# One attention-then-MoE kernel: a fixed GpSimd order, token numbers inside the sorted rows, two-head blocks for the last queries, and transposing DMAs for the MoE input

## The chip, the cores and the metric

One Trainium2 chip, one of its NeuronCores. The metric is device time in microseconds of one execution of the whole kernel. Engines are named as in the profile: PE (TensorE), PEld (its weight loads), DVE (VectorE), ACT (ScalarE), POOL (GpSimd), SP (SyncE). DMAs issued by POOL run in the software queue q0, those issued by SP in the hardware queue q1; both use the core's 16 DMA engines.

## The reference, cut to what matters

```python
# q, k, v: (8, 8, 576, 64); hidden 32
scores = q @ k.T / 8
pos = np.arange(S)
psi_rel = np.log1p(np.abs(pos[:, None] - pos[None, :]))
psi_i = np.log1p(np.maximum(pos[:, None], 1.0))
bias = np.maximum((psi_rel / psi_i)[..., None] @ w1 + b1, 0.0) @ w2     # (576, 576, 8 heads)
attn = softmax(scores + bias.transpose(2, 0, 1))
x = (attn @ v).transpose(0, 2, 1, 3).reshape(4608, 512)                 # tokens
for e in range(8):                                                      # one domain, one expert
    mask = domain_id == e
    out[mask] = np.maximum(x[mask] @ w1[e], 0.0) @ w2[e]                # 512 -> 1024 -> 512
```

## The kernel before, in words

**Stages.** The kernel runs five stages in turn. (1) Constants: `L4` holds logarithms of distances, `slope` one factor for each query row. (2) Position bias (`_phase_bias`): in 9 blocks `ib` of 64 queries, 16 tiles `hr` each (hidden units of 4 queries by 576 keys, 144 tiles in all, 36 buffers), PE multiplies them with `W2BIG` into `eb`, ACT evicts `eb` into the bias tables with Exp. (3) Routing (`_phase_route`): DVE computes for each token its row `posi` in an order sorted by expert (640 rows for each expert, a spill area behind). (4) Attention over 8 batches, 21 units each: PE writes scores `sc`, ACT takes the Exp into `e`, DVE multiplies by the bias, PE sums with v into `pu`, DVE normalizes (`norm`). Keys and queries 512 to 575 of each head are handled apart (`xl`, the last 64 queries). After the fourth head pair the finished rows `xt` are scattered by POOL's indirect DMAs into `fire_x`, a tensor in DRAM in sorted order, 4 scatters of 128 tokens and one of 64 for each batch. (5) MoE: for each expert 640 rows of `fire_x` are read as `xg`, transposed on PE into `xT`, then 64 matmuls into `hps` (Relu on ACT gives `hT`) and 40 into `ops`; DVE copies to `res`, and POOL scatters 5 blocks of 128 rows to the output by `sidx`, the token numbers of the sorted rows.

**Where `sidx` comes from.** `_phase_route` fills a DRAM tensor `fire_perm` by 40 indirect DMAs that write one 4-byte token number for each token, and reads it back once.

**What sets the order.** PE, DVE and ACT run in the order of the code. POOL's and SP's instructions are placed by the scheduler of the framework. One sequence of DMAs matters on SP: the zero fill of `fire_x` stands ahead of the second load of the domain numbers (`dom`), which the routing waits for. The expert weights come in through POOL (f32 to f16 in the DMA), two DMAs for each expert; experts 0 to 2 into the pool `wsb`, 3 to 6 into `wsb2`, 7 into `wsb` again.

Of the kernel before, what the change touches and what calls it, by code (L numbers as in the profile page):

```python
# [9 lines left out]
F32 = mybir.dt.float32  # L10
F16 = mybir.dt.float16
# [9 lines left out]
B = 8  # L21
# [9 lines left out]
PAD = 1 << 20  # L31

# [23 lines left out]
def _no_order(tc, key, inst):  # L56

    ins = inst.ins if hasattr(inst, "ins") else inst
    tc.declare_no_dep(ins, group=key, reason="rows of one permutation")
    tc.add_to_no_dep_group(key, ins)  # L60


def _setup_constants(tc, G, w1, b1, w2):
# [12 lines left out]
    nc.sync.dma_start(out=w1col, in_=bass.AP(tensor=w1.tensor, offset=0, ap=[[0, 4], [1, 32], [1, 1]]))  # L76
    G.nb1 = cst.tile([P, 1], F32, tag="nb1", name="nb1")
    nc.sync.dma_start(out=G.nb1, in_=bass.AP(tensor=b1.tensor, offset=0, ap=[[0, 4], [1, 32], [1, 1]]))
    nc.vector.tensor_scalar(out=G.nb1, in0=G.nb1, scalar1=-1.0, scalar2=None, op0=AO.mult)
# [9 lines left out]
    si = cst.tile([P, NGR], I32, tag="si", name="si")  # L89
    li = G.tmp.tile([P, W4 + W1], I32, tag="li", name="li")  # L90
    for g in range(4):
        pg = slice(32 * g, 32 * g + 32)

        nc.gpsimd.iota(si[pg, 0:128], base=4 * g, channel_multiplier=0, pattern=[[1, 4], [16, 32]])
        nc.gpsimd.iota(si[pg, 128:144], base=512 + g, channel_multiplier=0, pattern=[[4, 16]])
        nc.gpsimd.iota(li[pg, 0:W4], base=-(C4 + 4 * g), channel_multiplier=0, pattern=[[1, W4]])
        nc.gpsimd.iota(li[pg, W4:], base=-(C1 + 512 + g), channel_multiplier=0, pattern=[[1, W1]])
    G.slope = cst.tile([P, NGR], F32, tag="slope", name="slope")
    nc.vector.tensor_copy(out=G.slope, in_=si)
    nc.vector.tensor_scalar(out=G.slope, in0=G.slope, scalar1=1.0, scalar2=None, op0=AO.max)  # L100
    nc.scalar.activation(out=G.slope, in_=G.slope, func=AF.Ln, bias=1.0, scale=1.0)
    nc.vector.reciprocal(out=G.slope, in_=G.slope)
    nc.vector.tensor_scalar(out=G.slope, in0=G.slope, scalar1=w1col[:], scalar2=None, op0=AO.mult)
    lf = G.tmp.tile([P, W4 + W1], F32, tag="lf", name="lf")
    nc.vector.tensor_copy(out=lf, in_=li)
    nc.vector.scalar_tensor_tensor(out=lf, in0=lf, scalar=-1.0, in1=lf, op0=AO.mult, op1=AO.max)
    G.L4 = cst.tile([P, W4 + W1], F16, tag="L4", name="L4")
    nc.scalar.activation(out=G.L4, in_=lf, func=AF.Ln, bias=1.0, scale=1.0)  # L108


def _phase_bias(tc, G):
# [3 lines left out]
    with tc.tile_pool(name="fsb", bufs=1, side="right") as fsb, \  # L115
         tc.tile_pool(name="fps", bufs=1, space=bass.MemoryType.PSUM) as fps:
        for ib in range(9):
            hrl = []
            for k16 in range(16):
                if ib < 8:  # L120
                    r, a = ib // 2, 16 * (ib % 2) + k16
                    m, c0 = 32 * r + a, C4 - (16 * a + r)
                else:
                    m, c0 = 128 + k16, W4 + C1 - 4 * k16
                hr = fsb.tile([P, S], F16, tag="hr", name="hr", bufs=36)
                nc.vector.tensor_scalar(out=hr, in0=G.L4[:, c0: c0 + S],  # L126
                                        scalar1=G.slope[:, m: m + 1], scalar2=G.nb1[:],
                                        op0=AO.mult, op1=AO.max)
                hrl.append(hr)
            for jcs in ((0, 1), (2, 3), (4,)):  # L130
                eb = fps.tile([P, 2, 512], F32, tag="eb", name="eb", bufs=3)
                for k16 in range(16):
                    for lj, jc in enumerate(jcs):
# [5 lines left out]
                        else:  # L139
                            for h2 in range(2):  # L140
                                nc.tensor.matmul(
                                    out=eb[64 * h2: 64 * h2 + 64, lj, 32 * k16: 32 * k16 + 32],
                                    lhsT=hr[:, 512:576], rhs=G.W2BIG[:, 0:32], start=True, stop=True)
                ebv = eb.rearrange("p l (i h) -> p l h i", h=8)
                i0 = 64 * ib
                if jcs[0] == 4:
                    for h2 in range(2):
                        o = G.biasR[64 * h2: 64 * h2 + 64, :, i0: i0 + 64] if ib < 8 else \
                            G.biasRL[64 * h2: 64 * h2 + 64]
                        nc.scalar.activation(out=o, in_=ebv[64 * h2: 64 * h2 + 64, 0, h2::2, :],  # L150
# [16 lines left out]
def _phase_route(tc, G, moe_domain_id):  # L167
# [8 lines left out]
    G.perm_dram = nc.dram_tensor("fire_perm", (NSLOT, 1), I32, kind="Internal").ap()  # L176
# [100 lines left out]
    padt = pbuf.tile([P, NSLOT // P], I32, tag="padt", name="padt")  # L277
    nc.gpsimd.memset(padt, PAD)
    nc.sync.dma_start(out=G.perm_dram.rearrange("(p c) o -> p (c o)", p=P), in_=padt)
    nidx = pbuf.tile([P, B, NT], I32, tag="nidx", name="nidx")  # L280
    nc.gpsimd.iota(nidx[:, :, 0:4], base=0, channel_multiplier=4, pattern=[[S, B], [1, 4]])
    nc.gpsimd.iota(nidx[:, :, 4], base=512, channel_multiplier=1, pattern=[[S, B]])
# [8 lines left out]
    G.sidx = pbuf.tile([P, E * NCH, 1], I32, tag="sidx", name="sidx")  # L291
    nc.sync.dma_start(out=G.sidx, in_=bass.AP(tensor=G.perm_dram.tensor, offset=0,
                                              ap=[[1, 128], [128, E * NCH], [1, 1]]))


class _Attention:
# [443 lines left out]
```

## Time and profile before

| | us |
|---|---|
| median of 3 runs (range) | 527.84 (526.59 to 532.48) |
| the profiled execution, its own time | 523.68 |
| its span, first to last instruction | 522.0 |
| busy PE / DVE / ACT / POOL | 373.6 / 260.3 / 231.1 / 202.0 |

The profiled execution is 4.2 us under the median of the runs; its span is 1.7 us under its own time. No engine is busy for more than 72% of the span, and the shares are averages over stages with different limits: a stage is read by which wait ends last in it. Times in the rows further down count from the start of the span.

### The profile page before, as it was taken

How to read it: one execution, taken by the hardware profiler on the slowest of the kernel's cores; microseconds unless marked ns; L12 is line 12 of the kernel's file. 1: busy time of each engine (PE TensorE's matmuls, PEld its weight loads, DVE VectorE, ACT ScalarE, POOL GpSimd, SP SyncE). 2: the span in 40 equal slices, each digit the busy share in tenths (PEclk: the TensorE clock that was granted, in tenths of full speed). 3: DMA queues.
4: the chain of work that ended last, by engine and by line, in shares of the span. 5: the costliest groups of instructions: out<-in, count | busy, mean ns of one | idle time of the engine just before them, and what ended most of it. 6: DMA issues, size and time to landing. Idle time of an engine off the chain costs nothing. (4 is left out here: it accounts for less than half of the span.)

```text
span 522.0 us, 10886 instructions
## 1 busy us (share of the span) xinstructions
PE 373.6 (72%) x4578; PEld 235.3 (45%) x4578; DVE 260.3 (50%) x572; ACT 231.1 (44%) x290; POOL 202.0 (39%) x238
## 2 busy tenths in 40 slices
PE   0578844311298988889898977079639999999992
PEld 0366733100055555465555544055425566566550
DVE  5899985100369695777768674013022422422411
ACT  1444521000388987889697875021402143143140
POOL 9740445777606546543403042603013303313312
PEclk9999999555599999999897989579959999999997
DMA  0999987000992999979401010899998313102211
GB/s 3 155 233 366 319 123 131 2 0 0 99 155 53 161 203 149 151 124 114 77 3 46 4 46 21 160 241 241 215 246 206 112 50 123 69 22 88 81 39 73
DMA packets 79034, 61.39 MB, mean 118 GB/s; under 512 B 23558, under 2 KB 71430, under 8 KB 78984
## 3 DMA queue, kind: packets, MB, share of 16 engines
q0 software_dynamic: 56576, 45.12, 49.7%
q1 hardware_dynamic: 22408, 15.57, 10.8%
q8 instruction: 36, 0.59, 0.4%
q14 instruction: 14, 0.11, 0.1%
HBM read 67.17 MB, written 25.49 MB: 177 GB/s over the span
## 5 line engine op out<-in xcount | busy, mean ns | idle before, releaser
L412 ACT ACTIVATE e<-sc 128x1024 f16<-128x1024 f32 x168 | 156.7, 998 | 93.5 <-remote 67.2
L605 ACT ACTIVATE hT<-hps 128x640 f16<-128x640 f32 x64 | 45.1, 704 | 137.8 <-PE hps L601 136.2
L570 POOL DMA_INDIRECT out_dram<-res,sidx x40 | 39.5, 988 | 132.6 <-DVE res L569 131.9
L566 PE MATMUL ops<-w2e,hT 128*128 128x512 f16 x320 | 71.5, 383 | 0.0
L601 PE MATMUL hps<-xT,w1e 128*128 128x320 f16 x512 | 71.2, 300 | 0.0
L385 PE MATMUL sc<-qkT 64*128 64x512 f16 x256 | 54.3, 407 | 22.7 <-ACT e L412 16.7
L477 POOL DMA_INDIRECT fire_x<-xt,posi x32 | 34.4, 1076 | 81.2 <-DVE xt L459 71.0
L569 DVE COPY res<-ops 128x512 f32<-128x512 f32 x40 | 27.7, 691 | 76.2 <-PE ops L566 51.0
L417 DVE TENSOR_TENSOR e<-e,biasM 128x1024 f16<-128x1024 f16 x96 | 63.4, 685 | 3.3 <-ACT e L412 3.0
L601 PEld LDWEIGHTS <-w1e 128*128 128x128 f16 x512 | 50.3, 98 | 20.7
L136 PE MATMUL eb<-W2BIG,hr 128*128 128x32 f16 x576 | 36.0, 196 | 25.8 <-DVE hr L126 18.8
L433 PE MATMUL pu<-vext,e 128*128 128x65 f16 x1024 | 53.0, 199 | 0.0
L126 DVE TENSOR_SCALAR hr<-L,slope,nb 128x576 f16<-128x576 f16 x144 | 51.6, 435 | 1.7 <-ACT L L108 1.7
L561 DVE COPY xT<-pxt 128x512 f16<-128x512 f16 x40 | 15.8, 421 | 65.8 <-PE pxt L559 64.1
L566 PEld LDWEIGHTS <-hT 128*128 128x128 f16 x320 | 31.3, 99 | 36.8 <-issue 1.4
L287 POOL DMA_INDIRECT fire_perm<-nidx,posi x40 | 38.7, 969 | 21.0 <-issue 21.0
L433 PEld LDWEIGHTS <-e 128*128 128x128 f16 x1024 | 46.2, 102 | 0.0
L367 DVE COPY qkT<-pt 128x1024 f16<-128x1024 f16 x32 | 21.8, 683 | 47.7 <-remote 43.5
L136 PEld LDWEIGHTS <-hr 128*128 128x128 f16 x576 | 26.5, 117 | 34.7 <-DVE hr L126 17.6
L429 PE MATMUL pu<-vrag,e 128*128 128x130 f16 x128 | 29.9, 234 | 13.1 <-DVE xl L470 7.9
L559 PE MATMUL pxt<-idn,xg 128*128 128x128 f16 x160 | 15.1, 235 | 33.6 <-DMA xg<-fire_x 18.1
L345 PE MATMUL pt<-idn,qn 128*64 128x128 f16 x256 | 15.3, 249 | 27.1 <-DVE qkT L367 14.3
(123 smaller groups left out, 407.6 us busy)
## 6 DMA issues: line engine op xcount, KB each, us to landing
fire_x<-zero SPq DMA_DIRECT2D x1, 9984.0 KB, 37.0
w1e<-in_moe_w_dram POOLq DMA_DIRECT2D x8, 1024.0 KB
w2e<-in_moe_w_dram POOLq DMA_DIRECT2D x8, 1024.0 KB
xg<-fire_x SPq DMA_DIRECT2D x8, 640.0 KB, 8.6
qn<-in_q_dram POOLq DMA_DIRECT2D x8, 512.0 KB
kn<-in_k_dram POOLq DMA_DIRECT2D x8, 512.0 KB
vst<-in_v_dram POOLq DMA_DIRECT2D x8, 512.0 KB
fire_perm<-nidx,posi POOLq DMA_INDIRECT x40
```

The costliest lines, as they stand in the source:

```text
L126: nc.vector.tensor_scalar(out=hr, in0=G.L4[:, c0: c0 + S], scalar1=G.slope[:, m: m + 1], scalar2=G.nb1[:], op0=AO.mult, op1=AO.max)
L136: nc.tensor.matmul(out=eb[:, lj, 32 * k16: 32 * k16 + 32], lhsT=rap(hr, jc, [[4, 128]]), rhs=G.W2BIG[:, 0:32], start=True, stop=True)
L287: _no_order(tc, "slots", nc.gpsimd.indirect_dma_start(out=G.perm_dram[:, :], out_offset=bass.IndirectOffsetOnAxis(ap=G.posi[0:n, c:c + 1], ...
L385: mm(out=sc[:, h2, :], lhsT=self.qkT[b, p][hs[h2], 1, 128 * c: 128 * c + 128], rhs=self.qkT[b, p][hs[h2], 0, :], start=not raw, stop=True)
L412: nc.scalar.activation(out=ef[:, 0:n], in_=sf[:, 0:n], func=AF.Exp, bias=0.0, scale=0.125)
L417: self.nc.vector.tensor_tensor(out=job[0], in0=job[0], in1=job[1], op=AO.mult)
L433: mm(out=self.pu[:, c // 2, o + 65 * h2: o + 65 * h2 + 65], lhsT=self.e[b, ("m", p, j)][:, h2, 128 * c: 128 * c + 128], rhs=vx[:, 2 * p + ...
L477: _no_order(self.tc, "x_rows", self.nc.gpsimd.indirect_dma_start(out=self.x_dram[:, :], out_offset=bass.IndirectOffsetOnAxis(ap=self.G.pos ...
L566: nc.tensor.matmul(out=ops_, lhsT=hT[:, fc, t0: t0 + 128], rhs=w2e[:, fc, :], start=(fc == 0), stop=(fc == 7))
L570: _no_order(tc, "out_rows", nc.gpsimd.indirect_dma_start(out=out[:], out_offset=bass.IndirectOffsetOnAxis(ap=idx, axis=0), in_=res[:], in_ ...
L601: nc.tensor.matmul(out=hps[:, hf, 0:HC], lhsT=w1e[:, dc, 128 * fc: 128 * fc + 128], rhs=xT[:, dc, HC * hf: HC * hf + HC], start=(dc == 0), ...
L605: nc.scalar.activation(out=hT[:, fc, :].rearrange("p (a b) -> p a b", a=2), in_=hps[:, :, 0:HC], func=AF.Relu, bias=0.0, scale=1.0)
```

## The change

Six things change at once.

1. **Token numbers ride in the rows.** Rows of `fire_x` grow from 512 to 514 f16 (1024 to 1028 bytes); the last 4 bytes hold the token's number, written into `xt` and `xl` by a POOL iota (`new_rows`). `fire_perm`, its 40 scatters and `sidx` are gone; the MoE reads the numbers as `ids`. The zero fill writes 1028-byte rows too.
2. **Fixed GpSimd order.** A small class `_Issue` chains POOL's DMAs in the order of the code (scatters among themselves stay free).
3. **Expert weights later.** Experts 0 to 2 load during attention, as in the code before; 3 to 7 one at a time, each behind the first output scatter of the expert three places ahead, where before four of them were issued together ahead of the MoE.
4. **x by transposing DMAs.** For each expert four DMA transposes on SP (128 columns of 640 rows each) write `xT`; PE's 20 transposes and DVE's 5 copies for each expert go.
5. **Last queries in two-head blocks.** The 36 matmuls of `av` for the last 64 queries become 20 with full 128-row blocks; `norm` there runs in two halves. For the other head pairs its two multiplications become one.
6. **Constants and bias.** The iotas run over all partitions at once, the absolute value moves to ACT, 27 of the 144 `hr` tiles move from DVE to ACT, and each `eb` block of the last keys takes one matmul in place of two. `res` gets 6 buffers for 4.

```diff
+class _Issue:
+    def __call__(self, inst):
+        ins = _ins(inst)
+        for before in self.free or ([self.fixed] if self.fixed is not None else []):
+            self._behind(ins, before)
+        self.fixed, self.free = ins, []
+        return inst
+    def scatter(self, inst):
+        ins = _ins(inst)
+        if self.fixed is not None:
+            self._behind(ins, self.fixed)
+        self.free.append(ins)
+        return inst
...
+                if k16 in (3, 8, 13):
+                    nc.scalar.activation(out=hr, in_=G.L4[:, c0: c0 + S], func=AF.Relu,
+                                         bias=G.pb1[:], scale=G.slope[:, m: m + 1])
...
-    for bb in range(B):
-        for t in range(NT):
-            n = 128 if t < 4 else 64
-            c = NT * bb + t
-            _no_order(tc, "slots", nc.gpsimd.indirect_dma_start(
-                out=G.perm_dram[:, :],
-                out_offset=bass.IndirectOffsetOnAxis(ap=G.posi[0:n, c:c + 1], axis=0),
-                in_=nidx[0:n, bb, t:t + 1], in_offset=None))
...
+            h2, q = c // 2, 2 * (c % 2)
             ex = self.e[b, ("x",)]
+            out = self.pu[:, h2, o: o + 130].rearrange("p (q d) -> p q d", q=2)
+            mm(out=out, lhsT=ex[:, 0, 64 * q: 64 * q + 128],
+               rhs=vr[:, q: q + 2, 65 * h2: 65 * h2 + 65], start=True, stop=False, skip_group_check=True)
+            for j in range(4):
+                l0 = 256 * (j % 2) + 64 * q
+                mm(out=out, lhsT=self.e[b, ("l", j // 2)][:, h2, l0: l0 + 128],
+                   rhs=vx[:, 2 * q + h2: 2 * q + h2 + 3: 2, j, :], start=False, stop=(j == 3),
+                   skip_group_check=True)
...
+    def new_rows(self, tag, n, c, base, step):
+
+        t = self.G.asb.tile([n, c, XW], F16, tag=tag, name=tag, bufs=2)
+        self.G.issue(self.nc.gpsimd.iota(t[:, :, DM:].bitcast(I32), base=base, channel_multiplier=step,
+                                         pattern=[[1, c], [0, 1]]))
+        return t
...
     def fetch(e):
-        xg = msb.tile([P, NCH, DM], F16, tag="xg", name="xg", bufs=3)
-        nc.sync.dma_start(out=xg, in_=x_dram[e * CAP: e * CAP + CAP, :]
+        xT = msb.tile([P, 4, CAP], F16, tag="xT", name="xT", bufs=3)
+        for dc in range(4):
+            nc.sync.dma_start_transpose(out=xT[:, dc, :],
+                                        in_=x_dram[e * CAP: e * CAP + CAP, 128 * dc: 128 * dc + 128])
+        ids = msb.tile([P, NCH, 2], F16, tag="ids", name="ids", bufs=3)
+        nc.sync.dma_start(out=ids, in_=x_dram[e * CAP: e * CAP + CAP, DM:]
                           .rearrange("(k p) d -> p k d", p=128))
...
         for kk in range(NCH):
-            second(hT, 128 * kk, w2e, G.sidx[:, e * NCH + kk, :])
-        if e + G.NW + G.NW2 < E:
-            G.wts[e + G.NW + G.NW2] = _load_expert(nc, G.wsb, moe_w1, moe_w2, e + G.NW + G.NW2, G.NW)
+            second(hT, 128 * kk, w2e, ids[:, kk, :])
+            if kk == 0 and e + G.NW < E:
+                e2 = e + G.NW
+                pool, n = (G.wsb2, G.NW2) if e < G.NW2 else (G.wsb, G.NW)
+                G.wts[e2] = _load_expert(nc, pool, moe_w1, moe_w2, e2, n, G.issue)
...
+            nc.gpsimd.memset(zero[:, :, DM:].bitcast(I32), PAD)
             nc.sync.dma_start(out=x_dram.rearrange("(p c) d -> p c d", p=P),
-                              in_=zero.to_broadcast([P, NSLOT // P, DM]))
+                              in_=zero.to_broadcast([P, NSLOT // P, XW]))
```

**POOL between the bias and the first units of attention, before** (`qn`, `ql`, `kn`, `kl`, `vst`, `vrag` are loads of q, k and v; `w1e`, `w2e` of expert weights):

```order
L337 DMA vrag_126<-in_v_dram 64x4x64 x2
L541 DMA w1e<-in_moe_w_dram 128x4x1024
L325 DMA ql<-in_q_dram 64x8x64
L325 DMA kl<-in_k_dram 64x8x64
L543 DMA w2e<-in_moe_w_dram 128x8x512
L541 DMA w1e<-in_moe_w_dram 128x4x1024
L287 DMA fire_perm<-nidx,posi 9984x1 x40
L323 DMA qn<-in_q_dram 128x8x256
L323 DMA kn<-in_k_dram 128x8x256
```

POOL at the same place now:

```order
L297 MEMSET pb 128x672
L355 DMA qn<-in_q_dram 128x8x256
L358 DMA ql<-in_q_dram 64x8x64
L355 DMA kn<-in_k_dram 128x8x256
L358 DMA kl<-in_k_dram 64x8x64
L365 DMA vst<-in_v_dram 128x8x256
L372 DMA vrag_130<-in_v_dram 64x4x64 x2
L516 IOTA xt 128x4
```

The 40 scatters and the early weight loads are gone from here; the third batch's loads stand alone.

**POOL at the end of attention and in the MoE, before** (`out_dram` is the output; the fetch of x that the first expert waits for is SP's):

```order
L541 DMA w1e<-in_moe_w_dram 128x4x1024
L543 DMA w2e<-in_moe_w_dram 128x8x512
L570 DMA out_dram<-res,sidx 4608x512 x4
L541 DMA w1e<-in_moe_w_dram 128x4x1024
L570 DMA out_dram<-res,sidx 4608x512
L543 DMA w2e<-in_moe_w_dram 128x8x512
L570 DMA out_dram<-res,sidx 4608x512 x35
```

POOL at the same place now:

```order
L522 DMA fire_x<-xl,posi 9984x514
L606 DMA out_dram<-res,ids 4608x512
L588 DMA w1e<-in_moe_w_dram 128x4x1024
L590 DMA w2e<-in_moe_w_dram 128x8x512
L606 DMA out_dram<-res,ids 4608x512 x5
L588 DMA w1e<-in_moe_w_dram 128x4x1024
L590 DMA w2e<-in_moe_w_dram 128x8x512
```

Before, three more pairs of weight loads stand right ahead of the first of these rows; now each pair stands behind one output scatter.

**ACT in the constants and the first bias block, now** (before, it held one table load, two Ln, a second table load and then the evictions, with no `hr`):

```order
L135 ACT_TABLE_LOAD
L135 ACTIVATE lf<-li,gs 128x1075
L136 ACT_TABLE_LOAD
L136 ACTIVATE L_108<-lf 128x1075
L142 ACTIVATE slope<-slope 128x144
L154 ACTIVATE lf<-li,gs 128x636
L155 ACTIVATE L_108<-lf 128x636
L174 ACTIVATE hr<-L_108,pb_83,slope 128x576 x3
L203 ACT_TABLE_LOAD
L203 ACTIVATE biasM<-eb 128x2x6x64
```

One table load more, and three `hr` tiles ahead of each block's evictions: the `hr` of a block stand behind all evictions of the block before.

## Rows read from the trace of the kernel before

**Rows 1.** The page: busy tenths of PE in 40 slices of 13 us.

```profile
PE   0578844311298988889898977079639999999992
```

**Rows 2.** Busy time by stretch; the last three columns are granted clock, DMA share, GB/s.

```profile
39.00:52.00 13.00, 11.09 (x220) 8.82 (x221) 13.00 (x40) 5.85 (x13) 0.00 (x0) 1.00 1.13 365
...
91.00:104.00 13.00, 4.45 (x42) 2.44 (x39) 1.71 (x3) 1.06 (x2) 9.95 (x11) 0.50 0.02 2
...
330.00:340.00 10.00, 0.00 (x0) 0.00 (x0) 0.00 (x0) 0.00 (x0) 5.28 (x7) 0.50 1.05 192
...
350.00:400.00 50.00, 37.10 (x234) 22.00 (x233) 10.09 (x19) 9.82 (x15) 10.79 (x11) 0.86 1.14 238
```

**Rows 3.** Timeline of POOL: first and last of the 40 scatters to `fire_perm`.

```profile
82.87 1.05 POOL L287 DMA_INDIRECT fire_perm<-nidx,posi  x1 [9.15 <-issue]
...
132.60 0.90 POOL L287 DMA_INDIRECT fire_perm<-nidx,posi  x1 [0.30 <-issue]
```

**Rows 4.** Timeline of PE: scores of the fourth and fifth unit of attention.

```profile
94.54 0.61 PE L385 MATMUL sc<-qkT 64*128 64x512 f16 x2
...
102.14 0.58 PE L385 MATMUL sc<-qkT 64*128 64x512 f16 x1 [0.56 <-issue]
```

**Rows 5.** Timeline of ACT: the Exp of the fourth unit, and of the fifth and after.

```profile
116.20 1.02 ACT L412 ACTIVATE e<-sc 128x1024 f16<-128x1024 f32 x1 [20.87 <-remote]
139.42 4.87 ACT L412 ACTIVATE e<-sc 128x1024 f16<-128x1024 f32 x5 [22.19 <-remote]
```

**Rows 6.** Timeline of DVE: the `hr` tiles, first and last run.

```profile
16.00 44.13 DVE L126 TENSOR_SCALAR hr<-L,slope,nb 128x576 f16<-128x576 f16 x122 [1.70 <-ACT L L108]
...
59.72 7.92 DVE L126 TENSOR_SCALAR hr<-L,slope,nb 128x576 f16<-128x576 f16 x23
```

**Rows 7.** Timeline of ACT: the last evictions of the bias.

```profile
69.98 0.77 ACT L150 ACTIVATE biasRL<-eb 64x256 f16<-64x256 f32 x2
```

**Rows 8.** Groups of instructions by line and form: busy, mean ns, idle before.

```profile
L153 ACT ACTIVATE biasM<-eb 128x768 f16<-128x768 f32 x16 | 13.0, 811 | 25.9 <-PE eb L136 25.9
L156 ACT ACTIVATE biasM<-eb 128x256 f16<-128x256 f32 x16 | 6.1, 379 | 0.0
...
L470 DVE TENSOR_TENSOR xl<-pu,rz 64x512 f16<-64x512 f32 x8 | 5.5, 682 | 0.3
...
L101 ACT ACT_TABLE_LOAD x1 | 1.3, 1283 | 1.0 <-PEq L724 1.0
```

**Rows 9.** The eight fetches of x, from issue to landing.

```profile
DMA to landing us min/median/max: 4.3/8.6/23.6
```

**Rows 10.** The zero fill of `fire_x`: the page's DMA issues, then SP's timeline.

```profile
fire_x<-zero SPq DMA_DIRECT2D x1, 9984.0 KB, 37.0
...
27.35 0.65 SPq L694 DMA_DIRECT2D fire_x<-zero  x1
```

**Rows 11.** Timeline of DVE: end of the routing.

```profile
81.81 0.18 DVE L276 CAST posi<-posf 128x40 int32<-128x40 f32 x1
```

**Rows 12.** Timeline of ACT: where batches 1 and 7 of attention begin.

```profile
156.94 6.78 ACT L412 ACTIVATE e<-sc 128x1024 f16<-128x1024 f32 x7 [0.65 <-PE sc L391]
...
298.23 5.65 ACT L412 ACTIVATE e<-sc 128x1024 f16<-128x1024 f32 x6 [0.65 <-PE sc L391]
```

**Rows 13.** Timeline of SP: the fetches of x, from the first issue.

```profile
330.31 58.06 SPq L578 DMA_DIRECT2D xg<-fire_x  x6
```

**Rows 14.** Timeline of PE in the MoE: first expert, a stall, the last experts.

```profile
344.96 0.47 PE L601 MATMUL hps<-xT,w1e 128*128 128x320 f16 x1
...
386.29 1.69 PE L559 MATMUL pxt<-idn,xg 128*128 128x128 f16 x12 [12.33 <-DVE xT L561]
...
485.63 8.80 PE L566 MATMUL ops<-w2e,hT 128*128 128x512 f16 x40
...
502.96 8.80 PE L566 MATMUL ops<-w2e,hT 128*128 128x512 f16 x40
```

**Rows 15.** The software queue alone between 91 and 104 us: packets, MB, share.

```profile
q0 software_dynamic: 320, 0.01, 1.8%
```

More of the change, by code (lines that the diff above doesn't have):

```diff
@@ L31 @@
 PAD = 1 << 20
+XW = DM + 2
 NT = 5
@@ new lines, in _setup_constants @@
+    nc.gpsimd.iota(si[:, 128:144], base=512, channel_multiplier=0, pattern=[[4, 16]])
+    pf = cst.tile([P, 2], F32, tag="pf", name="pf")
+    nc.vector.tensor_copy(out=pf[:, 0:1], in_=pi)
+    g1 = cst.tile([P, 1], F32, tag="g1", name="g1")
+    nc.vector.tensor_scalar(out=g1, in0=pf[:, 0:1], scalar1=32.0, scalar2=None, op0=AO.is_ge)
+    for lim in (64.0, 96.0):
+        nc.vector.tensor_scalar(out=pf[:, 1:2], in0=pf[:, 0:1], scalar1=lim, scalar2=None, op0=AO.is_ge)
+        nc.vector.tensor_tensor(out=g1, in0=g1, in1=pf[:, 1:2], op=AO.add)
@@ new lines, in _setup_constants @@
+    gs = cst.tile([P, 3], F32, tag="gs", name="gs")
+    nc.vector.tensor_scalar(out=gs[:, 0:1], in0=g1, scalar1=4.0, scalar2=None, op0=AO.mult)
+    nc.vector.tensor_scalar(out=gs[:, 1:2], in0=g1, scalar1=-4.0, scalar2=None, op0=AO.mult)
+    nc.vector.tensor_scalar(out=gs[:, 2:3], in0=g1, scalar1=-1.0, scalar2=None, op0=AO.mult)
+    lf = G.tmp.tile([P, W4 + W1], F32, tag="lf", name="lf")
+    G.L4 = cst.tile([P, W4 + W1], F16, tag="L4", name="L4")
+    nc.scalar.activation(out=lf[:, 0:W4], in_=li[:, 0:W4], func=AF.Abs, bias=gs[:, 1:2], scale=1.0)
@@ new lines, in _setup_constants @@
+    nc.scalar.activation(out=G.L4[:, 0:W4], in_=lf[:, 0:W4], func=AF.Ln, bias=1.0, scale=1.0)
+    G.slope = cst.tile([P, NGR], F32, tag="slope", name="slope")
+    nc.vector.tensor_scalar(out=G.slope[:, 0:128], in0=si[:, 0:128], scalar1=gs[:, 0:1], scalar2=1.0,
+                            op0=AO.add, op1=AO.max)
+    nc.vector.tensor_scalar(out=G.slope[:, 128:], in0=si[:, 128:], scalar1=g1[:], scalar2=1.0,
+                            op0=AO.add, op1=AO.max)
+    nc.scalar.activation(out=G.slope, in_=G.slope, func=AF.Ln, bias=1.0, scale=1.0)
@@ L80, in _setup_constants @@
+    nc.vector.reciprocal(out=G.slope, in_=G.slope)
+    nc.vector.tensor_scalar(out=G.slope, in0=G.slope, scalar1=w1col[:], scalar2=None, op0=AO.mult)
     w2sb = cst.tile([HID, 8], F32, tag="w2sb", name="w2sb")
@@ L88, in _setup_constants @@
         )
[L89 to L108, printed above, removed]
+    nc.scalar.activation(out=lf[:, W4:], in_=li[:, W4:], func=AF.Abs, bias=gs[:, 2:3], scale=1.0)
+    nc.scalar.activation(out=G.L4[:, W4:], in_=lf[:, W4:], func=AF.Ln, bias=1.0, scale=1.0)
 def _phase_bias(tc, G):
@@ L139, in _phase_bias @@
                         else:
[L140 to L143, printed above, removed]
+                            nc.tensor.matmul(out=eb[0:64, lj, 32 * k16: 32 * k16 + 32],
+                                             lhsT=hr[:, 512:576],
+                                             rhs=G.W2BIG[:, 0:32], start=True, stop=True)
                 ebv = eb.rearrange("p l (i h) -> p l h i", h=8)
```

175 lines of the change are left out of this document (79 added, 96 removed).

## The prediction, made before the changed kernel ran

> **What bounds the kernel now.** I read the page's strip first, then the busy times by stretch, then the timelines inside the holes. The strip has two holes: PE is nearly idle from about 90 to 140 us, and again around 330 [rows 1]. Outside them three stages each have a limit of their own: the bias is paced by DVE's `hr` tiles, attention by ACT's Exp, the MoE by PE.
>
> *The first hole.* Routing ends with `posi` at 81.99 [rows 11], and the 40 scatters to `fire_perm` run on POOL from 82.87 to 133.50 [rows 3]. In that time attention has begun but crawls: between 91 and 104 us PE is busy 4.45 of 13 us, at the lower clock level (granted 0.50), and the DMA engines at 2% [rows 2]. The scores of the fourth unit end on PE at 95.15, its Exp starts at 116.20; those of the fifth end at 102.72, its Exp starts at 139.42 [rows 4, 5]. The Exp waits for nothing else that the program names, so PE's signal reaches ACT 21 and 37 us late. The lateness grows while the scatters run and ends 6 us after the last. From 139.42 on ACT takes five units without a gap [rows 5], and batch 1 starts at 156.94 [rows 12]. How a scatter holds back PE's signals no row shows; that it does is read from the coincidence.
>
> *The second hole.* The fetch of x is issued at 330.31, and the first MoE matmul starts at 344.96 [rows 13, 14]: 14.65 us, with PE at 0 [rows 2].
>
> *The MoE.* From the seventh expert's `ops` to the last one's is 17.33 us (485.63 to 502.96) [rows 14], and this step alone has no transposes in it; the other experts pay about 2 more. Once PE stands 12.33 us for a chain that ends in `res` waiting for an output scatter behind weight loads [rows 14]. The last `ops` end at 511.76 [rows 14]; 10.2 us of the span of 522.0 follow.
>
> **The change part by part**, against the profiled execution (span 522.0, own time 1.7 more).
>
> *Constants: 0.* `hr` starts at 16.00 [rows 6]. POOL's iotas get shorter, but ACT has one more table load (1.28 [rows 8]) in the chain before `slope`. I take no gain, with 2 us either way.
>
> *Bias: -3.9.* DVE does 13 of 16 tiles in each block at 0.36 (44.13 over 122 [rows 6]), later 0.34 (7.92 over 23). That alone would give 10 us. But ACT now holds three `hr` behind all evictions of the block before, and PE needs the first of them at its fourth tile. So the chain of a block runs through ACT. An `hr` of 576 columns is 0.65 by interpolation between 379 ns for 256 and 811 for 768 [rows 8], and about 0.55 from start to start. ACT's round is three `hr` (1.75), two pairs of evictions (1.06 each), the two of the last keys (0.77 [rows 7]) and two waits for PE of about 0.3: 5.3. Before, all ran from 16.00 to 70.75 [rows 6, 7], 54.75 us. Now: 4.7 for the first 13 tiles, 3.8 to the end of the first block's evictions (2.9 of them, and 0.9 for PE's last matmuls, an estimate), eight blocks at 5.3: 50.9. Ends: 0 (no gain) and -7 (5.0 a block).
>
> *Routing's own chain: 0.* It follows the bias as before, if `dom` has landed. `dom` queues behind the zero fill on SP: issued at 27.35 before, 37.0 us to landing [rows 10]; with POOL's shorter start it is issued at about 22 now. It is needed at about 62 and lands at 59 if 1028-byte rows cost what 1024-byte rows cost. This is a cover of 3 us, and a rival below.
>
> *The 40 scatters: -48.3.* Before, 74.95 us passed from `posi` (81.99) to batch 1 (156.94) [rows 11, 12]. Without the lateness: about 5 for the transposes and the first scores (an estimate), and 21 units at the pace at which the last 17 of them ran (139.42 to 156.94 [rows 5, 12]), 21.6: 26.6. What takes the scatters' place on POOL is the third batch's loads, not needed for another batch. Ends: 0 (the hole has another cause) and -50.
>
> *Attention's remaining batches: -2.* Batches 1 to 6 took 141.3 us (156.94 to 298.23) [rows 12], 23.5 each, against an ACT floor of 21 (20 Exp of 1.02 and a short one). The merged multiply saves DVE about 0.15 four times a batch (one of 512 elements is 0.68 [rows 8]), the split half for the last queries gives back 0.3, and 16 PE matmuls fewer lie mostly beside ACT. I take 0.3 a batch. Ends: -17 (every batch at the floor) and +14 (2 us a batch lost to POOL's rigid order). In that order each batch's q and k stand one whole batch ahead of use, behind at most one expert's weights; those two DMAs take 9 us at 238 GB/s [rows 2], so the cover is over 10 us.
>
> *The first fetch: -6.0.* Weights no longer stand in its way, since those of experts 0 to 2 are there. No row shows a transposing DMA. The nearest are the eight fetches of the same 655 KB: 4.3, 8.6 and 23.6 us [rows 9]. I take the median for four transposes: 8.6 for 14.65. Ends: -10 and +9.
>
> *The MoE: -27.0.* Before, 344.96 to 511.76 is 166.8. Now eight times 17.33 is 138.6, and 1.2 for the first expert at the lower clock: 139.8. This holds if the DMAs hide. With weights, an expert moves 2.10 MB of them, 1.31 MB of output and 0.66 MB of x: 4.07 MB in 17.33 us is 235 GB/s, against 238 measured at full DMA share [rows 2]. So the cover is thin for experts 0 to 4. Six `res` buffers and weights three experts ahead give about 10 us of slack.
>
> [...]
>
> *Sum:* -3.9 - 48.3 - 2 - 6.0 - 27.0 = -87.2; span 434.8, own time 436.5. The median of the runs lies 4.2 above the profiled execution, so about **440**.
>
> **The rivals.**
>
> 1. *Transposes fill the DMA engines.* If x moves in 32-byte pieces, an expert has 20,480 of them. A packet of 4 bytes held an engine for 11.7 ns (13 us, 16 engines, 1.8%, 320 packets [rows 15]), so 15 us of all 16 engines, beside 14.3 for 3.41 MB at 238: 29.3 in place of 17.33 for five experts, +60: **500**. Milder forms lie between 455 and 500. For it: DMA is already near full in that stretch. Against: nothing in the rows says how the pieces are cut.
>
> 2. *Slower: the transposes become the pace of the MoE.* If one transposing DMA uses one of the 16 engines (or its pieces are far smaller), 655 KB at a sixteenth of about 365 GB/s, which the zero fill reached between 39 and 52 us [rows 2], are 28.7 us an expert. First fetch issued at 275.7 (330.31 less the 54.2 to 54.6 won until then); eight such, then one expert's matmuls (17.3) and the end (10.2): 533 span, **539** as a median. It decides from 27.4 us an expert, 6.8 a DMA, on. Nothing queued behind could help, since SP issues them in order. Finer pieces would be far worse: at 2 bytes, 240 us an expert.
>
> 3. *The hole at 90 to 140 stays.* If the lateness comes from attention's cold start, not from the scatters, 48.3 comes back: **488**. Against: it ends when they end, and the units right after it run at full pace.
>
> 4. *The zero fill is dearer.* A row of 1028 bytes may be cut in two. At the 192 GB/s of a mixed stretch [rows 2], instead of 276 (10.2 MB in 37.0), it takes 53 us, `dom` lands at 75, and routing, attention and all behind start 12 us later: **452**.
>
> **How the numbers follow.** Chances: the forecast (425 to 455) 0.57; rival 1, all forms, 0.22; rival 2 0.07; rival 3 0.08; rival 4 0.06. The predicted time is the forecast's. From 425 to 500 leaves out rival 2, the worst of rival 1 and a gain in attention beyond 15 us, together under 0.2. A difference under 1%, 5 us, can't be told from none here. Faster by more: all but rival 2, 0.92; within 1%: 0.02, rival 2 just at its turning point; slower: 0.06.
>
> **What would show it.** Right: no hole after routing, the first Exp within 5 us of `posi`, batch 1 about 27 us after it; bias blocks 5.3 us apart with ACT's `hr` ending PE's waits; first `hps` about 12 us after the last scatter; 17.3 us from `ops` to `ops`, PE never waiting for `xT` after the first expert. Rival 1 shows as waits of PE or DVE on `w1e`, `res` or `xT` in experts 1 to 5 at full DMA share; rival 2 as PE waiting for `xT` before every expert with the DMAs idle; rival 3 as Exp late with POOL quiet; rival 4 as DVE waiting for `dom`. The forecast falls if POOL's fixed order makes attention wait for q, k or v, or if the transposes take more than 4.3 us each.

## The result and the profile after

The change makes the kernel faster: median 451.5 us (450.36 to 452.05) for 527.22, a ratio of 0.855 with the interval 0.8481 to 0.8618. The profiled execution took 450.36 us, its span is 448.8. The forecast was 440, so the kernel is 11.5 us slower than forecast. Some executions of a kernel run at a lower mean granted clock than its others and take longer: of e2 below one took 434.67 us at 0.975, the others 438.54 to 441.92 at 0.955 to 0.961.

The page of the kernel after, busy tenths in 40 slices of 11.2 us (compare [rows 1]): the hole around 90 to 140 us is gone, but a new one lies at 67 to 101 us.

```profile
PE   0566660128979888888888878339999999999992
...
DMA  4999999109919999999911000156999999991302
```

The new hole begins behind the bias. The timeline of SP of the kernel after, the zero fill and the second load of the domain numbers (`dom`) behind it (compare [rows 10]). The second figure of a row is the time that SP spends on it: 52.83 us for `dom`, where it was 31.70 before.

```profile
21.12 0.65 SPq L724 DMA_DIRECT2D fire_x<-zero  x1
21.82 52.83 SPq L232 DMA_DIRECT2D dom<-in_moe_domain_id_dram  x1
```

The timeline of DVE of the kernel after, first and last step of the routing (compare [rows 11]). In brackets stands the idle time ahead and what ended it: DVE waits 25.48 us for `dom`.

```profile
84.02 0.18 DVE L236 CAST domf<-dom 128x40 f32<-128x40 int32 x1 [25.48 <-DMA dom<-in_moe_domain_id_dram]
...
97.51 0.18 DVE L325 CAST posi<-posf 128x40 int32<-128x40 f32 x1
```

Busy time by stretch of the kernel after (columns as in [rows 2]): the fill has the DMA engines full, and yet moves 184 to 186 GB/s, where the one before reached 365 [rows 2]. The third line counts the DMA packets between 36 and 44 us: about 1.03 KB each and none under 512 B, so no row of 1028 bytes is cut in two.

```profile
36.00:44.00 8.00, 6.06 (x138) 5.61 (x138) 8.00 (x25) 7.12 (x14) 0.00 (x0) 1.00 1.11 184
...
52.00:65.00 13.00, 8.61 (x190) 7.65 (x189) 4.83 (x14) 11.61 (x20) 0.00 (x0) 1.00 1.11 186
...
DMA packets 1418, 1.47 MB, mean 184 GB/s; under 512 B 0, under 2 KB 1417, under 8 KB 1417
```

The timeline of ACT of the kernel after: end of the bias, first Exp, starts of batches 1 and 7 (compare [rows 7, 12]).

```profile
67.09 0.76 ACT L200 ACTIVATE biasRL<-eb 64x256 f16<-64x256 f32 x2
101.97 2.86 ACT L447 ACTIVATE e<-sc 128x1024 f16<-128x1024 f32 x3 [34.13 <-PE sc L426]
...
123.19 6.56 ACT L447 ACTIVATE e<-sc 128x1024 f16<-128x1024 f32 x7 [0.59 <-PE sc L426]
...
261.60 8.60 ACT L447 ACTIVATE e<-sc 128x1024 f16<-128x1024 f32 x9 [0.58 <-PE sc L426]
```

The first fetch of x on SP's timeline of the kernel after (compare [rows 13]):

```profile
293.44 5.17 SPq L615 DMA_TRANSPOSE xT<-fire_x  x4
```

The MoE on PE's timeline of the kernel after (compare [rows 14]): four waits for the first `xT`, then six steps of 17.33 us from `ops` to `ops` and a last one of 17.53, without a stall.

```profile
296.39 0.45 PE L631 MATMUL hps<-xT,w1e 128*128 128x320 f16 x1 [10.15 <-DMA xT<-fire_x]
297.74 0.42 PE L631 MATMUL hps<-xT,w1e 128*128 128x320 f16 x1 [0.90 <-DMA xT<-fire_x]
299.04 0.43 PE L631 MATMUL hps<-xT,w1e 128*128 128x320 f16 x1 [0.88 <-DMA xT<-fire_x]
300.20 9.87 PE L631 MATMUL hps<-xT,w1e 128*128 128x320 f16 x61 [0.74 <-DMA xT<-fire_x]
309.91 8.80 PE L602 MATMUL ops<-w2e,hT 128*128 128x512 f16 x40
...
431.40 8.80 PE L602 MATMUL ops<-w2e,hT 128*128 128x512 f16 x40
```

From these starts and ends, the span by stretches (us):

| stretch | before | after | difference | forecast |
|---|---|---|---|---|
| to the end of the bias | 70.75 | 67.85 | -2.9 | -3.9 |
| bias to `posi` | 11.24 | 29.84 | **+18.6** | 0 |
| `posi` to batch 1 | 74.95 | 25.50 | -49.4 | -48.3 |
| batches 1 to 6 | 141.29 | 138.41 | -2.9 | -2 |
| batch 7 to the fetch's issue | 32.08 | 31.84 | -0.2 | (in the line above) |
| fetch's issue to the last `ops` | 181.45 | 146.76 | -34.7 | -33.0 |
| the end | 10.24 | 8.60 | -1.6 | 0 |
| sum | 522.0 | 448.8 | -73.2 | -87.2 |

### The profile page after: what moved, and what is told of

Read it like the earlier page. It is cut to its first block, busy times and chain, and to the rows that moved or that the text cites. A ratio compares the mean times of both kernels' runs of the same rounds, so it can differ in the third digit from the quotient of the medians.

```text
span 448.8 us, 9956 instructions
## 1 busy us (share of the span) xinstructions
PE 340.5 (76%) x4146; PEld 213.3 (48%) x4146; DVE 231.7 (52%) x496; ACT 254.5 (57%) x321; POOL 152.3 (34%) x201
## 5 line engine op out<-in xcount | busy, mean ns | idle before, releaser
L605 DVE COPY res<-ops 128x512 f32<-128x512 f32 x40 | 27.7, 691 | 125.7 <-PE ops L602 122.5
L606 POOL DMA_INDIRECT out_dram<-res,ids x40 | 40.0, 999 | 101.6 <-DVE res L605 94.8
L420 PE MATMUL sc<-qkT 64*128 64x512 f16 x256 | 50.0, 385 | 8.8 <-ACT e L447 8.7
L187 PE MATMUL eb<-W2BIG,hr 128*128 128x32 f16 x576 | 26.9, 194 | 31.4 <-ACT hr L174 15.5
L469 PE MATMUL pu<-vext,e 128*128 128x65 f16 x1024 | 50.6, 194 | 0.1
L469 PEld LDWEIGHTS <-e 128*128 128x128 f16 x1024 | 43.7, 98 | 0.1
L177 DVE TENSOR_SCALAR hr<-L,slope,nb 128x576 f16<-128x576 f16 x117 | 41.7, 433 | 2.6 <-PE eb L191 2.6
L187 PEld LDWEIGHTS <-hr 128*128 128x128 f16 x576 | 22.3, 116 | 35.4 <-ACT hr L174 17.9
L355 POOL DMA_DIRECT2D qn<-in_q_dram x8 | 7.4, 924 | 85.0 <-PE pt L380 85.0
L420 PEld LDWEIGHTS <-qkT 64*128 64x128 f16 x256 | 13.7, 92 | 31.8 <-issue 25.1
L465 PEld LDWEIGHTS <-e 128*128 128x128 f16 x128 | 12.3, 96 | 32.1 <-issue 17.9
L380 PE MATMUL pt<-idn,qn 128*64 128x128 f16 x256 | 14.4, 235 | 11.5 <-DVE qkTl L402 10.8
L493 DVE TENSOR_TENSOR xt<-pu,rz 128x512 f16<-128x512 f32 x32 | 22.1, 692 | 1.4
```

Of the source, the lines that this page charges most:

```text
L177: nc.vector.tensor_scalar(out=hr, in0=G.L4[:, c0: c0 + S], scalar1=G.slope[:, m: m + 1], scalar2=G.nb1[:], op0=AO.mult, op1=AO.max)
L187: nc.tensor.matmul(out=eb[:, lj, 32 * k16: 32 * k16 + 32], lhsT=rap(hr, jc, [[4, 128]]), rhs=G.W2BIG[:, 0:32], start=True, stop=True)
L420: mm(out=sc[:, h2, :], lhsT=self.qkT[b, p][hs[h2], 1, 128 * c: 128 * c + 128], rhs=self.qkT[b, p][hs[h2], 0, :], start=not raw, stop=True)
L465: mm(out=self.pu[:, c // 2, o: o + 130], lhsT=er[:, p % 2, 128 * c: 128 * c + 128], rhs=vr[:, p, :], start=True, stop=False, skip_group_ch ...
L469: mm(out=self.pu[:, c // 2, o + 65 * h2: o + 65 * h2 + 65], lhsT=self.e[b, ("m", p, j)][:, h2, 128 * c: 128 * c + 128], rhs=vx[:, 2 * p + ...
L606: inst = nc.gpsimd.indirect_dma_start(out=out[:], out_offset=bass.IndirectOffsetOnAxis(ap=idx.bitcast(I32), axis=0), in_=res[:], in_offset ...
```

## The experiments

The theory that the runs were to test: the forecast's mechanisms hold, and one term was wrong, the cover of `dom` behind the zero fill. Edits are to the kernel after (e4: to the kernel before). The kernel before ran beside every group.

### The zero fill

**e1: the domain numbers first.** Both loads of `dom` are issued at the very start.

```diff
+                _load_dom(tc, G, moe_domain_id)
                 _setup_constants(tc, G, w1, b1, w2)
```

> The changed kernel with both loads of the domain numbers issued ahead of the zero fill; nothing else moved. Theory (the missing 11.5 us are the zero fill holding back the domain numbers): the DVE cast of the domain numbers starts when DVE's hr tiles end, posi is ready about 10 us after the bias (67.85 plus 11, so about 79 for 97.7), batch 1 and everything behind comes about 18 us earlier, 433 us. Rival (the late routing is a matter of the bias stage, or the first scatters of attention wait for the zero fill anyway): under 5 us won, 447 to 452.

**e2: rows of 1088 bytes.**

```diff
-XW = DM + 2
+XW = DM + 32
...
```

> The changed kernel with rows of fire_x of 1088 bytes (a multiple of 64) in place of 1028; the zero fill and the scatters write the whole row. Theory A (rows that start off a 64-byte boundary cost double): the fill runs at about 276 GB/s or more again, 10.9 MB in about 39 us, the domain numbers land near 61, 432 to 436 us. Theory B (any row that is longer than 1024 bytes costs a second piece): the fill stays at about 190 GB/s, 450 us or more. Theory C (the fill only shares the engines with the loads of q, k and v): as B, about 451.

**e3: a wider source for the fill.**

```diff
-            zero = G.cst.tile([P, 1, XW], F16, tag="zero", name="zero")
...
+                zero = zp.tile([P, 6, XW], F16, tag="zero", name="zero")
```

> The changed kernel with the 1028-byte rows kept, but the zero tile six rows wide, so that the fill writes pieces of 6168 contiguous bytes. Theory A (the cost is per row that starts off a boundary): a sixth of the odd starts, 37 to 42 us for the fill, 432 to 437 us. Theory B (a second piece for each row): also gone, the same time, 432 to 437. Theory C (the fill only shares the engines with the loads): about 451. If the cost is for every byte written off a boundary, also 451.

**e5: the kernel after once more.** No edit.

> The changed kernel as it is, beside the others of this group on one chip. Theory: what e1 and e3 won over it (17.7 and 16.4 us of span) is the edit's and not the chip's, so this kernel is again 16 to 19 us above them, about 451 us. Rival (a quicker chip): under 446 us.

Measured: e1 433.24 us (0.8325, 0.8285 to 0.8364), e3 433.81 (0.8333, 0.8298 to 0.8368), e5 450.71 (0.8591, 0.8564 to 0.8619). Spans: 431.1, 432.4 and 450.1. e2 has 441.46 as a median (0.8482, 0.8448 to 0.8516), above the 432 to 436 expected; its profiled execution, 434.67 us with a span of 433.1, lies within them.

Busy time between 36 and 44 us, of e1, then e2, then e3 (the last column is GB/s):

```profile
36.00:44.00 8.00, 5.67 (x130) 5.15 (x131) 8.00 (x24) 7.02 (x14) 0.00 (x0) 1.00 1.09 201
```

```profile
36.00:44.00 8.00, 6.05 (x140) 5.59 (x138) 8.00 (x25) 7.24 (x14) 0.00 (x0) 1.00 1.12 350
```

```profile
36.00:44.00 8.00, 4.99 (x108) 4.41 (x109) 8.00 (x25) 7.16 (x12) 0.00 (x0) 1.00 1.03 389
```

e1 leaves the fill as slow as it was and wins all the same: the fill costs time only through `dom` behind it. In e2 rows that are 60 bytes longer go through at 350 GB/s, so length isn't it (theory B). Nor is it the company of other loads (C): in the kernel after all but one of the 1418 packets of this stretch are of the fill's queue. What is left is a row off a 64-byte boundary (A). In these tensors a row that starts off one also ends off one, and no run separates the two. In e3 a sixth as many pieces lie so, and the price is gone. e1 and e3, with nothing in common but an early `dom`, agree within 0.6 us.

### The scatters and the hole before

**e4: the kernel before without its 40 scatters.**

```diff
-            _no_order(tc, "slots", nc.gpsimd.indirect_dma_start(
-                out=G.perm_dram[:, :],
...
+    nc.sync.dma_start(out=bass.AP(tensor=G.perm_dram.tensor, offset=0, ap=[[40, 128], [1, 40]]),
+                      in_=nidx.rearrange("p b t -> p (b t)"))
```

> The kernel before with the 40 scatters to fire_perm left out; one plain DMA writes the token numbers in token order in their place (so output rows go to other tokens; the padding rows stay 512). Theory (the scatters on POOL hold back PE's signals): the hole between 90 and 140 us closes, 48 us less, about 479 us. Rival (attention's cold start makes the hole): 522 to 528 us, the Exps of units five and six as late as before.

**e6: e1 with 40 scatters put back.**

```diff
+    for c in range(NCOL):
...
+        inst = nc.gpsimd.indirect_dma_start(
+            out=dummy[:, :], out_offset=bass.IndirectOffsetOnAxis(ap=G.posi[0:n, c:c + 1], axis=0),
+            in_=nidx[0:n, c:c + 1], in_offset=None)
+        G.issue(inst)
```

> e1 (domain numbers loaded first) with 40 indirect 4-byte scatters put back on POOL behind posi, into a spare tensor that nobody reads. Theory (POOL's indirect DMAs hold back PE's signals while they run back to back): the hole opens again, posi to batch 1 takes about 74 us for 25.7, 481 us. Rival (the hole before came from the scheduler's order on POOL or from the read-back of sidx, not from the scatters): 433 to 438 us.

**e7: e1 with 40 plain DMAs in that place.**

```diff
+    for c in range(NCOL):
...
+        inst = nc.gpsimd.dma_start(out=dummy[128 * c: 128 * c + n, :], in_=nidx[0:n, 0:1])
+        G.issue(inst)
```

> As e6, but the 40 are plain DMAs of POOL with the same 4-byte pieces (64 or 128 of them each), not indirect ones. Theory (it takes an indirect DMA on POOL): no hole, at most 3 us lost, 433 to 437 us. Rival A (any DMA that POOL writes holds back PE's signals): POOL is busy for 40 times 0.7 to 0.9 us, the hole is 28 to 36 us, 461 to 470 us. Rival B (the 4-byte pieces do it, on the DMA engines): about 481 us as in e6.

Measured: e4 470.48 us (0.9048, 0.9007 to 0.9089), 50 us under the kernel before; the first Exp comes at 86.66, 4.2 us behind `posi` (82.47), and batch 1 at 108.00. e6 493.01 (487.35 to 498.22), with 77 us from `posi` to batch 1 for 25.5. e7 467.6 (0.8921, 0.8888 to 0.8953).

The timeline of ACT of e4, first Exp and start of batch 1:

```profile
86.66 2.85 ACT L407 ACTIVATE e<-sc 128x1024 f16<-128x1024 f32 x3 [15.85 <-PE sc L386]
...
108.00 4.69 ACT L407 ACTIVATE e<-sc 128x1024 f16<-128x1024 f32 x5 [0.65 <-PE sc L386]
```

The timeline of PE of e6, while POOL's scatters run from 80.62 to 130.91: for a stretch PE's own instructions come out one by one, 2.8 us apart, with no producer to wait for ("issue").

```profile
114.07 0.27 PE L396 MATMUL pt<-idn,kn 128*64 128x128 f16 x1 [1.79 <-issue]
116.87 0.27 PE L396 MATMUL pt<-idn,kn 128*64 128x128 f16 x1 [2.53 <-issue]
119.67 0.58 PE L436 MATMUL sc<-qkT 64*128 64x512 f16 x1 [2.53 <-issue]
122.47 0.58 PE L436 MATMUL sc<-qkT 64*128 64x512 f16 x1 [2.22 <-issue]
```

The timeline of ACT of e6: the next Exp is 43 us late ("remote": the profile names no instruction that released it).

```profile
92.92 1.02 ACT L463 ACTIVATE e<-sc 128x1024 f16<-128x1024 f32 x1 [3.11 <-issue]
137.30 1.94 ACT L463 ACTIVATE e<-sc 128x1024 f16<-128x1024 f32 x2 [43.36 <-remote]
```

Taken out of one kernel and put into the other, the scatters move the same stretch by about 50 us: rival 3 is out. e7's time was that of its rival A (461 to 470), but its trace says otherwise. The timelines of e7, first ACT, then POOL, then PE:

```profile
88.66 7.48 ACT L461 ACTIVATE e<-sc 128x1024 f16<-128x1024 f32 x8 [0.73 <-PE pt L394]
```

```profile
119.28 0.94 POOL L369 DMA_DIRECT2D qn<-in_q_dram  x1 [2.24 <-DMA spare<-nidx]
```

```profile
131.14 0.39 PE L394 MATMUL ptl<-idn,ql 64*128 64x64 f16 x4 [21.21 <-DMA ql<-in_q_dram]
```

Beside the plain DMAs eight Exps run without a gap; the signals are late by 3.35 us at most. What costs is the queue: the third batch's loads stand behind the 40, `qn` is issued at 119.28, and PE waits 21.21 us for `ql`. So of 40 DMAs with 4-byte pieces only the indirect ones held PE back, as the theory had it (they also write to scattered places, the plain ones to places in order, which isn't separated), and I had priced e7 without what is queued behind.

This bears on the 50 us too. In the kernel before (`qn` and `kn`) and in e6 the third batch's loads also stood behind the 40 scatters. e7's queue alone cost 34.9 us of span with POOL held until 119.28; in e6 it is held until 130.91. So most of the 50 us might have been lost even with PE's signals on time. The runs show what the scatters cost, and the traces that PE's signals were late; what the lateness alone costs isn't shown.

### The bias and the routing

**e8: e1 with two `hr` on ACT.**

```diff
-                if k16 in (3, 8, 13):
+                if k16 in (5, 11):
```

> e1 with two of 16 hr tiles of each bias block on ACT (the sixth and the twelfth) in place of three. Theory (the block is paced by ACT's chain, whose hr are 0.8 us each): ACT's round falls from 5.63 to 4.85, DVE's 14 tiles take 4.8, eight blocks win 6 us, 427 us. Rival (the pace is PE's or the wait of ACT for it): 0 to 2 us won, 431 to 433.

Measured: 432.29 us (428.68 to 434.01; 0.8254, 0.8223 to 0.8284). The timeline of ACT of e8, last evictions of two blocks in a row, and the end of the bias:

```profile
33.48 0.76 ACT L200 ACTIVATE biasR<-eb 64x256 f16<-64x256 f32 x2
...
38.47 0.76 ACT L200 ACTIVATE biasR<-eb 64x256 f16<-64x256 f32 x2
...
64.61 0.76 ACT L200 ACTIVATE biasRL<-eb 64x256 f16<-64x256 f32 x2
```

A block takes 4.99 us where it took 5.63, the bias ends at 65.37 for 68.29, and the span of the profiled execution falls by 4.0: ACT's chain paced the bias, though not all of the 6 us came, since the other blocks take 5.0 to 6.0. For the whole kernel the gain isn't clear of the spread: the median is 1.0 us under e1's, which is what the rival expected, and the ranges (428.68 to 434.01 and 431.89 to 434.43) overlap.

**e9: e1 with the routing spread over the bias.** `_phase_route` becomes a generator with a `yield` behind each DVE instruction.

```diff
+                    if ib:
+                        done += 1
+                        if done % 2:
+                            next(route, None)
                 hrl.append(hr)
```

> e1 with DVE's 48 routing instructions spread over the bias stage, one behind every second hr tile from the second block on, and the prefix matmul (app) ahead of the third block on PE; what is computed stays the same. Theory (once the domain numbers are there, routing's own chain of about 12 us between bias and attention sets attention's start, and DVE has 9 us to spare under the bias, since ACT paces it): the bias ends 0 to 3 us later than 68.3, the first Exp comes 4 to 5 us behind it in place of 15.6, span 420 to 424, 422 to 426 us. Rival (DVE becomes the pace of the bias, as it has nothing to spare): the bias ends 10 to 12 us later and nothing is won, 432 to 436 us.

Measured: **426.54 us** (0.8185, 0.8154 to 0.8216), the fastest version here and ahead of the kernels before and after; three executions took 425.85 to 427.04, one 437.03. The timeline of ACT of e9: end of the bias and first Exp.

```profile
70.41 0.76 ACT L205 ACTIVATE biasRL<-eb 64x256 f16<-64x256 f32 x2
75.63 2.86 ACT L498 ACTIVATE e<-sc 128x1024 f16<-128x1024 f32 x3 [4.47 <-PE sc L477]
```

ACT idles 4.47 us there, for 15.60 in e1. The bias ends 2.9 later, the first Exp comes 8.3 earlier, and the span falls by 5.6: two steps of the MoE, 17.99 and 18.98 us for 17.33, take 2.3 back.

**e12: e9 with two more edits.**

```diff
-                    if ib:
+                    if ib > 1:
                         done += 1
-                        if done % 2:
+                        if done % 13 % 2:
...
+            eng = nc.scalar if e == 0 and dc % 2 else nc.sync
+            eng.dma_start_transpose(
```

> e9 with two more edits: the routing instructions start with the third bias block in place of the second (six of them behind every 13 hr tiles of DVE), and the first expert's second and fourth transposing DMA are issued by ACT, which is idle there, in place of SP. Theory (in e9 the second and third block were paced by DVE, 7.0 us each, before it had any lead; and an issuing queue takes 1.3 us for a transposing DMA, which sets when the first expert's x is complete): the bias ends 1 to 2.5 us earlier, the first expert's matmuls reach full rate about 2 us sooner behind the last Exp, 421 to 424 us. Rival (DVE falls behind later instead, and the DMA engines, not the queue, set the pace of the transposes): 425 to 428 us, as e9.

Measured: 433.29 us (0.8281, 0.8245 to 0.8317), slower than e9. The timelines of e12, ACT, SP and PE at the first fetch:

```profile
269.42 7.12 ACTq L667 DMA_TRANSPOSE xT<-fire_x  x2
```

```profile
272.38 6.94 SPq L667 DMA_TRANSPOSE xT<-fire_x  x2
```

```profile
280.98 11.31 PE L683 MATMUL hps<-xT,w1e 128*128 128x320 f16 x62 [4.92 <-DMA xT<-fire_x]
```

The four transposing DMAs don't overlap: SP's first is issued 2.96 us after ACT's first, and the four take 9.9 us to issue, where one queue issued them in 5.2. The queues take turns (ACT at 269.42 and 275.38, SP at 272.38 and 278.19), each about 3 us behind the other: SP's two stand 2.9 and 4.5 us waiting for a DMA into `xT`, and ACT's second comes between them. PE comes to full rate 13.3 us behind the last scatter (267.69), in e9 8.6. The pace of the bias did what was expected (end at 69.16 for 71.17), but batch 0 took 24.3 us for 21.8. The stretch of 10 us in it, of e12, then e9, shows a granted clock of 0.66 for 1.00 and ACT busy 7.91 us for 9.16:

```profile
80.00:90.00 10.00, 9.41 (x102) 5.07 (x102) 7.99 (x14) 7.91 (x9) 2.49 (x3) 0.66 1.54 171
```

```profile
80.00:90.00 10.00, 8.27 (x115) 4.67 (x115) 9.02 (x17) 9.16 (x10) 1.97 (x4) 1.00 1.62 175
```

PE had been busy 2.81 of the 5 us before in e12, 3.94 in e9. Why the clock fell stays open. Of e12's 6.0 us of span over e9, the stretch from the last Exp to the first `ops` lost 6.3 and batch 0 2.5; an earlier first Exp (1.1) and a quicker MoE gave the rest back. So e12 doesn't test the routing edit by itself.

### Two parts undone

**e10: e1 with PE's transposes.**

```diff
+            nc.tensor.transpose(out=pxt[:, dc, :],
+                                in_=xg[:, 128 * dc: 128 * dc + 128], identity=G.idn)
...
-            nc.sync.dma_start_transpose(out=xT[:, dc, :],
...
```

> e1 with part 4 of the change undone: x is fetched in plain rows and transposed by 20 PE matmuls and copied by 5 DVE instructions for each expert, as before. Theory (the transposing DMAs are hidden and take 2 us of PE from every expert): the ops to ops step is 19.3 for 17.33 in seven steps, 14 us, and the first expert's start is within 3 us of e1's, 445 to 449 us. Rival (the transposing DMAs load the DMA engines so much that plain fetches give time back elsewhere, or the first fetch gains more): 433 to 440 us.

Measured: 446.89 us (0.859, 0.8562 to 0.8618), 13.7 above e1, beside the same time of the kernel before (520.79). The timeline of PE of e10: the first expert's transposes, and the step from one `ops` to the next.

```profile
279.59 2.81 PE L621 MATMUL pxt<-idn,xg 128*128 128x128 f16 x20 [11.59 <-DMA xg<-fire_x]
...
294.14 8.80 PE L608 MATMUL ops<-w2e,hT 128*128 128x512 f16 x40
...
313.49 8.80 PE L608 MATMUL ops<-w2e,hT 128*128 128x512 f16 x40
```

Six steps are 19.35 us for 17.33, which makes 12.1, and the first `ops` start 2.0 later than in e1 (292.15): 14.1 us, the whole difference of the spans. Part 4 of the change is worth 14 us, on PE.

**e11: e1 with POOL's order left to the scheduler.**

```diff
     def __call__(self, inst):
-        ins = _ins(inst)
-        for before in self.free or ([self.fixed] if self.fixed is not None else []):
-            self._behind(ins, before)
-        self.fixed, self.free = ins, []
         return inst
```

> e1 with part 2 of the change undone: POOL's DMAs stand where the scheduler puts them (the weights of experts 0 and 1 and half of expert 2 ahead of most loads of the third batch). Theory (the fixed order is worth next to nothing in attention, since q, k and v stand a batch ahead of their use in both): 430 to 437 us. Rival (the weights delay q and k of the third batch, as the loads behind 40 plain DMAs were late in e7): 440 us or more, with PE waiting for ql or qn in the second batch.

Measured: 460.96 us (0.8873, 0.8836 to 0.891), 27.7 above e1. Batch 1 takes 7.6 us more, with ACT 7.35 late at one point, as the rival says; but the later batches are no slower (22.6 to 22.8 us for 22.7 to 23.0). The rest is elsewhere. POOL's timeline of e11, the last scatter into `fire_x`, and what the scheduler put right behind it:

```profile
279.46 0.90 POOL L520 DMA_INDIRECT fire_x<-xl,posi  x1 [0.30 <-issue]
280.36 0.82 POOL L586 DMA_DIRECT2D w1e<-in_moe_w_dram  x1
281.16 0.97 POOL L588 DMA_DIRECT2D w2e<-in_moe_w_dram  x1
```

Two more such pairs follow. PE's timeline of e11, the first expert:

```profile
292.75 0.45 PE L629 MATMUL hps<-xT,w1e 128*128 128x320 f16 x1 [17.76 <-DMA xT<-fire_x]
297.61 0.43 PE L629 MATMUL hps<-xT,w1e 128*128 128x320 f16 x1 [4.41 <-DMA xT<-fire_x]
303.69 0.43 PE L629 MATMUL hps<-xT,w1e 128*128 128x320 f16 x1 [5.66 <-DMA xT<-fire_x]
308.05 10.60 PE L629 MATMUL hps<-xT,w1e 128*128 128x320 f16 x61 [3.93 <-DMA xT<-fire_x]
```

From the last scatter's end (280.36) to full rate 27.7 us pass; in e1 it is 8.6 (273.88 to 282.48). Three experts' weights (issued from 280.36 on, the transposes from 282.04) share the DMA engines with the transposes (90% or more busy from 287 us on, by the page of e11): that costs 19 of the 27.7 us between the two kernels. My theory, next to nothing, fails: the fixed order is what keeps the weights out of the first fetch's way.

## Why the prediction was right, and where it missed

- **The 40 scatters** (-48.3): right in cause and size, -49.4. e4 and e6 show it both ways. That PE's late signals are the whole of it isn't shown: e7's queue alone cost 34.9.
- **Routing's own chain** (0, "provided `dom` has landed"): the step that failed. The sum took the cover of 3 us as enough, with 1028-byte rows at the price of 1024-byte rows. The runs showed rows off a 64-byte boundary at 184 to 201 GB/s in its place. Rival 4 (+12, chance 0.06) is what happened in effect, and larger: not 53 us, but 62 from SP's issue (21.82) to the cast (84.02). Its reason, a row cut in two, didn't happen: the packets are whole rows. It cost 18.6 us; e1 takes 17.7 of span back by moving one small load.
- **The bias** (-3.9): the chain through ACT was right, the size wrong. The interpolation between two kinds of eviction was too low: three `hr` take 2.38 us, not 1.75, and a block 5.63, not 5.3; the earlier start of DVE's `hr` (14.24 for 16.00) made up for part. e8 shows ACT's share.
- **Attention** (-2): -2.9 for six batches, but as far as the runs show by luck. e4, the kernel before without the scatters, has none of parts 2 and 5 and takes 135.06 us for the same six batches (108.00 to 243.06, granted clock 1.00), 3.35 less than the kernel after. Before, batches 5 and 6 ran at a lower granted clock (0.93 and 0.87 in the rows below) and took 49.8 us, where they take 45.0 in e4: more than the gain. Parts 5 and 6 weren't undone by themselves, so what they are worth isn't shown. The bound of +14 for the rigid order wasn't needed: undone, it costs 7.6 in batch 1 and gives 1.2 back in the six batches behind it (e11).

```profile
248.43:272.83 24.40, 21.55 (x343) 13.22 (x343) 18.06 (x37) 19.44 (x21) 6.35 (x7) 0.93 0.19 38
272.83:298.23 25.40, 22.72 (x343) 13.71 (x343) 18.11 (x37) 19.86 (x21) 5.14 (x5) 0.87 0.08 25
```

- **First fetch and MoE** (-33.0 together): -34.7. The fetch was over-priced (8.6; it takes 2.95 us to the first matmul and 6.76 to full rate), the steps of 17.33 right but for the last of 17.53. From the first matmul on, the MoE took 143.8 us for 139.8, mostly by the three further waits for the first `xT`. The reason given, that weights no longer stand in the way, holds, but it takes POOL's fixed order to keep the later loads late (e11).
- **Rivals 1 and 2** are out: under load an expert's four transposing DMAs take 13.1 to 15.2 us on SP, hidden behind 17.33. The first expert's four DMAs of 128x640, with only SP's queue on the DMA engines, have landed 6.8 us after the first issue (293.44 to 300.20). PE's 20 transposes for the first expert of e10 take 2.81 us, 0.14 each.
- **The median** lies 1.1 us above the profiled execution, not 4.2: 3.1 us of the 14 missed were given back there, by luck.

## What to carry to other kernels

When the length of a row changes, ask what waits behind the transfer in its queue, and give it a pitch that keeps the starts on a 64-byte boundary (here 350 GB/s for 184 to 201) or issue the small loads first. Before many indirect DMAs go out back to back on POOL, ask who needs PE's signals at that time (beside 40 of them an Exp came 43 us late in e6), and whose loads stand behind them in POOL's queue (34.9 us in e7, with plain DMAs). A fixed order on a DMA-issuing engine is priced where stages meet, by what the scheduler would have put there, not by the steady state (in e11 7.6 us in batch 1 and 19 at the first fetch, for 1.2 the other way in the six batches between).

## What the runs showed of the hardware

- DRAM writes of 1028-byte rows, laid end to end so that most start and end off a 64-byte boundary, ran at 184 to 201 GB/s with the DMA engines full; rows of 1088 bytes at 350, pieces of 6168 at 389. Beside the rows of 1024 bytes of the kernel before (365) that is nearly twice the time for a byte, and rows at multiples of 64 show hardly any of it (350). Whether a smaller multiple would do, and whether the start or the end of a row costs, wasn't tried.
- Back-to-back indirect DMAs of POOL (1.27 us each in the kernel before) delayed PE's own instructions, in one stretch of e6 to one in 2.8 us, and signals between the engines until 6 us after the last scatter (130.91 to 137.25 in e6, with POOL's plain loads in between). Plain DMAs with the same 4-byte pieces held them up by 3.35 us at most (e7). How is open.
- Transposing DMAs took longer in company: PE's waits between the first expert's pieces are 0.7 to 0.9 us in the kernel after, and 3.9 to 5.7 beside weight loads (e11).
